# Gate buffers ordered by their whole size, the scratch of the weight sums in another place, and a floating place in PE's list for the spread maxima

## The chip, the cores and the metric

The kernel is one program on 1 core of one Trainium2 chip. The metric is the device time of one execution in microseconds (us); the time of a kernel is the median of its runs. PE is the matrix engine, DVE the vector engine, ACT the scalar engine, POOL the GpSimd engine and SP the engine that issues the DMAs. L1263 is line 1263 of the kernel before; where the changed kernel has other line numbers, the text still speaks of lines of the kernel before, unless it says otherwise.

## The reference

Three parts run one after the other in float32. The attention has 4 batches, 8 heads, 576 positions and 64 features a head; the two dense parts work on its 4 x 576 = 2304 tokens of 512 features.

```python
def _attn_ref(q, k, v, s):
    scores = scale * np.matmul(q, k.transpose(0, 1, 3, 2))
    cum = np.cumsum(np.maximum(s, 0.0), axis=-1)
    bias = -(cum[:, :, :, None] - cum[:, :, None, :])
    scores = np.where(causal, -1000000000.0, scores + np.minimum(bias, 0.0))
    attn = softmax(scores)
    return np.matmul(attn, v)

def _moe_ref(x, w_in, w_out):        # 512 -> 2048 -> 512
    h = x @ w_in
    g = h * np.cos(h)
    return g @ w_out

def _moe2_ref(x, w1, w2, w3, w_out): # 512 -> 768 -> 512
    h = np.maximum(np.maximum(x @ w1, x @ w2), x @ w3)
    return h @ w_out
```

## The kernel before

**How the order comes about.** The program adds operations to a list planner (`P.add`): each with an engine, a planned duration, a key, and the byte spans that it reads and writes. Overlapping spans become dependences. The planner then simulates the engines with these durations and puts, whenever an engine is free, the ready operation of the smallest key on its list. Each engine issues its list in that order and waits at the head of it, so a late operand holds up everything behind. `P.flex` adds an operation with several choices of engine; each choice carries a number of microseconds by which it counts as ready later than it is. The evacuations (L891) choose in this way between ACT (L893) and DVE (L895). Matmuls of PE that are given through `link` keep the order in which they were linked.

**Operands.** A float32 operand is scaled by a power of two and split into two float16 halves, high and low; a product is three matmuls (high x high, high x low, low x high). ACT writes the high half (L402 for gates, L501 for operands) and DVE the low half (L432, L504).

**The power of two (`power`, L475).** The largest magnitude of each of 128 partitions is reduced on DVE (L479), cut to its power (L482, L485) and put on a diagonal (L488, into one buffer `dip_b`); PE multiplies that by ones (L491), so that all partitions see all maxima, and DVE reduces the bank (L494) and inverts (L496). This chain is called a spread of the maxima here. It is used in attention, for the gates (`gate_scale`), for each token block (`x_operands`, L1113) and each half of the weights (`w_operands`, L1156).

**The stages.** Attention runs in 32 steps. Beside its last ones PE computes h = x w_in in blocks of 320 or 256 tokens (L922, the projection); L893 on ACT evacuates it into one of three buffers `hs_b`, and SP stores it to the DRAM tensor `h_dram` (L440).

The gate stage (L1224) follows. It runs over five slabs of tokens, slab 0 of 256 and slabs 1 to 4 of 512, and in each over 16 chunks of h, one of 128 of the 2048 features. A chunk is loaded from `h_dram` (into one of 5 buffers `hl_b`); ACT rounds h / 2 pi to an integer (L1244, 3 buffers `kq_b`), DVE takes the remainder (L1246, 5 buffers `gl_b`), ACT the sine (L1249), DVE multiplies by h (L1252); L402 and L432 make the halves (8 buffers `gh_b`); PE runs 12 matmuls into four banks that it keeps for the whole slab (L1263). At a slab's end the banks are evacuated to `x2_b` by L893 or L895.

In between stand pieces for the next stage. `w_value` loads a piece of the third layer's weights, from 64-bit words, and rebuilds the values on DVE (L449, L452, L455) in one of three buffers `val_b`, with a maximum (L1152). `w_operands` makes the sums of weight pieces (L1167) in a scratch `ws4_b` and their halves (L501, L504). `x_operands` takes the maxima of a token block (L1118), the differences (L1128, scratch `sum_b`) and the halves. In slab 2 `w_operands(0)` and `x_operands(0)` stand side by side.

The product stage computes x w1, x w2 and x w3 by a scheme of 7 products in place of 8, in 27 groups (weight half, token block, which w). A product is 6 matmuls of 384 columns (L1336); ACT keeps the first ones of a group (L1344), DVE adds the others to them (L1361). The second and third `w_operands` and the last `x_operands` stand inside it. The last product with the second w_out (L1300) ends the kernel.

**Memory.** `hl_b`, `kq_b`, `gl_b` and `gh_b` are cut out of memory in which attention kept probabilities and exponentials, in pieces of 2048 bytes; of slab 0 only the first 1024 bytes of each are in use. `val_b` and `ws4_b` lie over x operands and over the three store buffers `hs_b` of h: the third of `val_b` over the one whose store is the last, `ws4_b` over the other two. The lines that decide it:

```python
    sum_b = place(3 * 4 * TB).parts(3)
    val_b = [Buf(nc, tail0 + 4096 * m, 4096) for m in range(3)]
    ws4_b = Buf(nc, tail0 + 3 * 4096, 3072)
    ...
            hs_, ks_, ls_ = ([z.span(0, 4 * n)] for z in (hb, kb, lb))
```

Of the kernel before, what the change touches and what calls it, by code (L numbers as in the profile page):

```python
# [13 lines left out]
BF16 = mybir.dt.bfloat16  # L14
# [17 lines left out]
NC2 = DFF2 // 128  # L32
# [8 lines left out]
TB = 384  # L41
# [280 lines left out]
def attn_moe_kernel(ctx, tc, qT, kT, v, s, w_in, w_out, w1, w2, w3, wo2, out):  # L322
    nc = tc.nc
# [7 lines left out]
    P = Plan()  # L331
# [24 lines left out]
    wg_b = [alloc(32) for _ in range(NC1 // G)]  # L356
# [3 lines left out]
    tail0 = used[0]  # L360
    x_b = [alloc(NPAIR * 2 * RANGES[r][1] * 2).ring(NPAIR) for r in range(2)]
    hs_b = alloc(3 * 2560).ring(3)
    tail1 = used[0]
# [15 lines left out]
    warm_b = alloc(256)  # L379
    dip_b = alloc(256)  # L380
# [93 lines left out]

    def power(col, given, small, key, z, unit=2.0 ** -14):  # L475


        a, sp, o, os_ = small.ap(F32, 8), [small.span()], bank(z)[:, 0:128], [bspan(z)]
# [11 lines left out]
            op0=ALU.mult), reads=sp + [eye_b.span()], writes=[dip_b.span()])  # L490
        P.add("PE", 0.07, key, lambda: nc.tensor.matmul(  # L491
            o, warm_b.ap(BF16, 128), dip_b.ap(BF16, 128), start=True, stop=True),
            reads=[warm_b.span(), dip_b.span()], writes=os_)
# [94 lines left out]
    for h in range(2):  # L588
        z = tri[64 * h:128, S - 64:]
# [425 lines left out]
    for st in range(len(STEPS)):  # L1015
# [16 lines left out]
        if st in WI_AT:  # L1032
            i_ = WI_AT.index(st)
            for c in range(NC1 * i_ // len(WI_AT), NC1 * (i_ + 1) // len(WI_AT)):
# [4 lines left out]
                small = wg_b[c // G]  # L1039
# [30 lines left out]
    def place(size):  # L1070
        z = Buf(nc, low[0], size)
        low[0] += size
        assert low[0] <= low_end
        return z
# [3 lines left out]
    w0_b, xo_b, xo1_b = place(WB), place(XB), place(XB)  # L1078
    sum_b = place(3 * 4 * TB).parts(3)
    val_b = [Buf(nc, tail0 + 4096 * m, 4096) for m in range(3)]  # L1080
    ws4_b = Buf(nc, tail0 + 3 * 4096, 3072)
    assert 3 * 4096 + 3072 <= tail1 - tail0
    gates0 = rest_b[0].lo
# [29 lines left out]
    def x_operands(tp, key, z):  # L1113
# [3 lines left out]
        for i in range(4):  # L1117
# [3 lines left out]
                reads=[x2_b[tp].span(8 * TB * i, 8 * TB)], writes=[small.span()])  # L1121
        power(4, small, small, key, z, 2.0 ** -12)
        by, bsp = small.ap(F32, 8)[:, 7:8], [small.span()]
# [32 lines left out]
    def w_operands(fp, key, z):  # L1156


        small = mn_b[fp]
        power(6, wg_b[fp], small, key, z, 2.0 ** -12)  # L1160
        by, bsp = small.ap(F32, 8)[:, 7:8], [small.span()]
# [22 lines left out]
    def out_values(key):  # L1184

        top, small = am_b[0], am_b[1]
        for f in range(NC2):
# [10 lines left out]
                reads=[top.span(), mn_b[f // 2].span()], writes=[top.span()])  # L1198
        power(NC2, top, small, key, 7)

# [23 lines left out]
    for t in range(-(-NT // 512)):  # L1224
# [5 lines left out]
        for c in range(NC1):  # L1230
# [9 lines left out]
            gt, lr, gs_, gl_s = two(gb, n)  # L1240
            hs_, ks_, ls_ = ([z.span(0, 4 * n)] for z in (hb, kb, lb))
            load(ht, h_dram[:, c, col0:col0 + n], 512 * n, key - 3,
# [210 lines left out]
T0_BANKS = 1  # L1453
WO_FROM = 8
WO_KEY = 300
WM_KEY = 200
# [83 lines left out]
```

## Time and profile before

| | us |
|---|---|
| median of 3 runs (lowest, highest) | 845.21 (842.23, 846.32) |
| the profiled execution: time | 843.37 |
| its span from first to last instruction | 841.6 |
| PE busy | 798.6 (95%) |
| DVE busy | 691.0 (82%) |
| ACT busy | 542.8 (64%) |
| POOL busy | 51.1 (6%) |

The profiled execution's own time is 1.8 us over its span, and its mean granted clock was 0.984 of full speed. It is 1.84 us under the median of the runs.

Two views are used ahead of the result. A row of the instructions in order of time gives start, length, engine, line, operation, output<-input with their sizes, and how many instructions of the kind ran one behind the other; in brackets stand the idle time of the engine before the row and what ended it. SPq is SP issuing a DMA. A row's length reaches some 0.08 us into the next row's, since instructions are pipelined; from start to start is the step. A row of busy time by stretch gives the stretch, its length, the busy time (and the instructions) of PE, PE's weight loads, DVE, ACT and POOL, then the granted clock of PE, the share of time of the DMA engines and GB/s.

### The profile page before, as it was taken

To read this page: it belongs to the slowest core of one execution; us is meant where nothing else is said; L and a number is where in the kernel's file an instruction comes from. 1 tells how busy PE (TensorE), PEld (TensorE's weight loads), DVE (VectorE), ACT (ScalarE), POOL (GpSimd) and SP (SyncE) were. 2 spreads that over 40 slices of the span, in tenths; PEclk is the share of its full clock that TensorE was granted. 3 is DMA by queue.
4 is the path that set the end of the run, shared out by engine and by line. 5 is a ranking of instruction groups with operands and counts; after the bars stand their busy time and mean duration, and the time that the engine had idled before them with its cause. 6 is when DMAs were issued, how large, how long until landed. Compare 5 with 4: busy or idle time off the path is not lost.

```text
span 841.6 us, 16200 instructions
## 1 busy us (share of the span) xinstructions
PE 798.6 (95%) x5905; PEld 504.1 (60%) x5905; DVE 691.0 (82%) x1677; ACT 542.8 (64%) x1173; POOL 51.1 (6%) x80
## 2 busy tenths in 40 slices
PE   7988589999999999899997989999999999999998
PEld 4666466788778768778543434444566666555554
DVE  7999989987987898588999999999999999613120
ACT  2787778988888889458976789962562533322121
POOL 4511112001000100000000000000000000000000
PEclk9899989999999999999999899999999999999999
DMA  8689978999999999955453134403003120010112
GB/s 250 141 192 220 220 184 223 223 210 216 240 175 211 240 172 221 263 167 167 140 160 113 51 101 128 148 13 125 26 1 100 51 90 12 1 42 35 38 38 75
DMA packets 154571, 114.14 MB, mean 136 GB/s; under 512 B 109662, under 2 KB 132446, under 8 KB 154492
## 3 DMA queue, kind: packets, MB, share of 16 engines
q1 hardware_dynamic: 154492, 113.11, 53.6%
q8 instruction: 46, 0.75, 0.4%
q14 instruction: 33, 0.27, 0.1%
HBM read 63.13 MB, written 23.74 MB: 103 GB/s over the span
## 4 chain that ended last, share of the span: by engine, by line
PE 50%; DVE 32%; DMA 7%; ACT 5%; issue 3%; SPq 1%; POOL 1%; POOLq 0%; DVEq 0%; ACTq 0%
PE banks L1336 21%; PE banks L922 14%; PE banks L1300 8%; DVE p L432 8%; DVE p L1252 4%; DVE p L1246 4%; PE banks L708 3%; PE banks L774 3%; DVE p L721 3%; DVE p L504 2%; ACT p L402 2%; DMA p<-h_dram 2%; DVE p L452 2%; DVE p L455 1%; DMA p<-in_moe_w_out_dram 1%
## 5 line engine op out<-in xcount | busy, mean ns | idle before, releaser
L922 PE MATMUL banks<-p,p 128*128 128x256 f16 (+1 forms) x1536 | 204.6, 289 | 13.1 <-ACT p L893 5.1
L1263 PE MATMUL banks<-p,p 128*128 128x512 f16 (+1 forms) x960 | 189.9, 360 | 2.5 <-DVE p L432 1.4
L1336 PE MATMUL banks<-p,p 128*128 128x384 f16 x1134 | 185.6, 326 | 1.1 <-DVE p L485 1.1
L922 PEld LDWEIGHTS <-p 128*128 128x128 f16 x1536 | 146.0, 99 | 61.6 <-issue 14.9
L402 ACT ACTIVATE p<-p,p 128x512 f16<-128x512 f32 (+4 forms) x241 | 143.1, 625 | 48.1 <-DVE p L1252 16.6
L432 DVE SCALAR_TENSOR_TENSOR p<-p,p,p 128x512 f16<-128x512 f32 (+4 forms) x244 | 153.7, 656 | 11.1 <-ACT p L402 10.4
L1263 PEld LDWEIGHTS <-p 128*128 128x128 f16 x960 | 94.3, 98 | 103.1 <-issue 12.5
L1336 PEld LDWEIGHTS <-p 128*128 128x128 f16 x1134 | 110.8, 98 | 74.9 <-issue 1.3
L893 ACT ACTIVATE p<-banks,p 128x256 f32<-128x256 f32 (+2 forms) x166 | 84.8, 520 | 100.2 <-PE banks L1300 61.6
L727 ACT ACTIVATE p<-p,p 128x128 f32<-128x128 f32 (+4 forms) x144 | 82.9, 576 | 19.4 <-DVE p L721 17.7
L1344 ACT ACTIVATE p<-banks 128x384 f32<-128x384 f32 x90 | 43.9, 488 | 73.2 <-PE banks L1336 71.7
L721 DVE CUSTOM_DVE_ANT_0 p<-banks,p 128x128 f32<-128x128 f32 (+4 forms) x144 | 71.6, 512 | 2.2 <-POOL p L417 0.5
L1300 PE MATMUL banks<-p,p 128*128 128x512 f16 (+1 forms) x342 | 71.0, 368 | 0.0
L1361 DVE TENSOR_TENSOR p<-banks,p 128x384 f32<-128x384 f32 x81 | 44.0, 550 | 30.7 <-PE banks L1336 30.3
L501 ACT ACTIVATE p<-p,p 128x512 f16<-128x512 f32 (+2 forms) x73 | 54.1, 783 | 15.9 <-DVE p L1167 3.9
L504 DVE SCALAR_TENSOR_TENSOR p<-p,p,p 128x512 f16<-128x512 f32 (+2 forms) x73 | 59.0, 830 | 6.0 <-ACT p L501 6.0
L1300 PEld LDWEIGHTS <-p 128*128 128x128 f16 x342 | 33.5, 98 | 36.1
L1249 ACT ACTIVATE p<-p,p 128x512 f32<-128x512 f32 (+1 forms) x80 | 51.6, 669 | 5.3 <-DVE p L1246 5.2
L708 PE MATMUL banks<-r,r 64*128 64x256 f32 (+3 forms) x360 | 48.3, 345 | 2.6 <-DVE p L721 1.4
L1252 DVE TENSOR_TENSOR p<-p,p 128x512 f32<-128x512 f32 (+1 forms) x80 | 49.1, 632 | 0.6 <-ACT p L1249 0.6
L1246 DVE SCALAR_TENSOR_TENSOR p<-p,p 128x512 f32<-128x512 int32 (+1 forms) x80 | 48.8, 631 | 0.0
L1244 ACT ACTIVATE p<-p 128x512 int32<-128x512 f32 (+1 forms) x80 | 44.5, 575 | 2.7 <-DMA p<-h_dram 2.5
(100 smaller groups left out, 776.1 us busy)
## 6 DMA issues: line engine op xcount, KB each, us to landing
p<-h_dram SPq DMA_DIRECT2D x64, 256.0 KB
p<-in_moe_w_out_dram SPq DMA_DIRECT2D x22, 512.0 KB
h_dram<-p SPq DMA_DIRECT2D x32, 320.0 KB
p<-in_moe_w_dram SPq DMA_DIRECT2D x18, 512.0 KB
p<-in_moe_w_in_dram SPq DMA_DIRECT2D x16, 512.0 KB
h_dram<-p SPq DMA_DIRECT2D x32, 256.0 KB
p<-in_k_dram SPq DMA_DIRECT2D x16, 288.0 KB
out_dram<-p SPq DMA_DIRECT2D x17, 256.0 KB
```

Source lines behind the costliest of these rows:

```text
L402: "ACT": (slow(cols, 0.19 if par else 0.09), lambda: nc.scalar.activation(out=out, in_=src, func=AF.Copy, scale=by)),
L432: n = P.add("DVEP", dve1(cols) + 0.06, key, lambda: nc.vector.scalar_tensor_tensor(out=lo, in0=src, scalar=by, in1=hi, op0=ALU.mult, op1=A ...
L504: P.add("DVEP", dve1(cols) + 0.06, key, lambda: nc.vector.scalar_tensor_tensor(out=lo, in0=src_, scalar=by, in1=hr, op0=ALU.mult, op1=ALU. ...
L721: nc.vector.tensor_tensor_reduce(out=e, in0=sc, in1=km, op0=ALU.add, op1=ALU.min, scale=-0.125, scalar=3.0e38, accum_out=mn[:, j:j + 1]),
L727: "ACT", act(n, 0.28), tg, lambda j=j, e=e, mn=mn, sm=sm: nc.scalar.activation(out=e, in_=e, func=AF.Exp, scale=-1.0, bias=mn[:, j:j + 1], ...
L893: "ACT": (act(cols, 0.05 if by is None else 0.15), lambda: nc.scalar.activation(out=out, in_=src, func=AF.Copy, scale=1.0 if by is None el ...
L922: nc.tensor.matmul(hp, w[:, wp, ks], xx, start=(k == 0 and m == 0), stop=(k == KD - 1 and m == 2),)
L1246: P.add("DVEP", dve1(n), key, lambda kt=kt, ht=ht, lt=lt: nc.vector.scalar_tensor_tensor(out=lt, in0=kt, scalar=-TWO_PI, in1=ht, op0=ALU.m ...
L1252: P.add("DVEP", dve1(n), key, lambda ht=ht, lt=lt: nc.vector.tensor_tensor(out=lt, in0=lt, in1=ht, op=ALU.mult), reads=hs_ + ls_, writes=ls_)
L1263: nc.tensor.matmul(bank(base + d)[:, 0:n], w[:, wp, ds], xx, start=(c == 0 and z == 0), stop=(c == NC1 - 1 and z == 2))
L1300: nc.tensor.matmul(o, hv[hp], wv[:, wp, c0:c1], start=(f == 0 and m == 0), stop=(f == NC2 - 1 and m == 2))
L1336: nc.tensor.matmul(bank(z)[:, 0:TB], w_, x_, start=(opens and j == 0 and k == 0), stop=(j == 1 and k == 2), skip_group_check=True)
```

## The change

Three edits.

- In the gate stage the spans of the buffers of loaded h, of integers and of remainders (`hs_`, `ks_`, `ls_`) are the whole 2048 bytes in each slab, not the part that a chunk fills. Only slab 0 fills less than the whole. Its operations are ordered behind whatever attention kept in the second half of a buffer too.
- The scratch of the weight sums, `ws4_b`, is the first 3072 bytes of the scratch `sum_b` of the x operands, and no longer lies over `hs_b`.
- The matmul of a spread (L491) is added through `flex` with one engine and a margin: in the calls of `x_operands`, `w_operands` and `out_operands` the planner counts it as ready 2.0 us later than its operands are. The margin is 0 elsewhere. The instruction itself is the same.

The diff:

```diff
--- before.py
+++ after.py
@@ -472,7 +472,7 @@
         P.after(m, [rows_out, *after])
         return raw.ap(I64, cols).bitcast(I32).rearrange("p (n two) -> p n two", two=2)
 
-    def power(col, given, small, key, z, unit=2.0 ** -14):
+    def power(col, given, small, key, z, unit=2.0 ** -14, margin=0.0):
 
 
         a, sp, o, os_ = small.ap(F32, 8), [small.span()], bank(z)[:, 0:128], [bspan(z)]
@@ -488,8 +488,8 @@
         P.add("DVEP", dve2(128) + 0.06, key, lambda: nc.vector.tensor_scalar(
             out=dip_b.ap(BF16, 128), in0=eye_b.ap(F32, 128), scalar1=a[:, 5:6], scalar2=None,
             op0=ALU.mult), reads=sp + [eye_b.span()], writes=[dip_b.span()])
-        P.add("PE", 0.07, key, lambda: nc.tensor.matmul(
-            o, warm_b.ap(BF16, 128), dip_b.ap(BF16, 128), start=True, stop=True),
+        P.flex(key, [("PE", 0.07, lambda: nc.tensor.matmul(
+            o, warm_b.ap(BF16, 128), dip_b.ap(BF16, 128), start=True, stop=True), margin)],
             reads=[warm_b.span(), dip_b.span()], writes=os_)
         P.add("DVE", dve1(128), key, lambda: nc.vector.tensor_reduce(
             out=a[:, 6:7], in_=o, op=ALU.max, axis=AX.X), reads=sp + os_, writes=sp)
@@ -1076,10 +1076,10 @@
     WB = 7 * 256 * 4 * 3
     XB = 7 * 2 * TB * 4
     w0_b, xo_b, xo1_b = place(WB), place(XB), place(XB)
-    sum_b = place(3 * 4 * TB).parts(3)
+    sums = place(3 * 4 * TB)
+    sum_b, ws4_b = sums.parts(3), sums.part(0, 3072)
     val_b = [Buf(nc, tail0 + 4096 * m, 4096) for m in range(3)]
-    ws4_b = Buf(nc, tail0 + 3 * 4096, 3072)
-    assert 3 * 4096 + 3072 <= tail1 - tail0
+    assert 3 * 4096 <= tail1 - tail0
     gates0 = rest_b[0].lo
     xo2_b, w1_b = Buf(nc, gates0, XB), Buf(nc, gates0 + XB, WB)
     assert XB + WB <= 21 * 2048 <= const0 - e0
@@ -1119,7 +1119,7 @@
                 out=small.ap(F32, 8)[:, i:i + 1], in_=x2_b[tp].ap(F32, 2 * TB, 8 * TB * i), op=ALU.max,
                 axis=AX.X, apply_absolute_value=True),
                 reads=[x2_b[tp].span(8 * TB * i, 8 * TB)], writes=[small.span()])
-        power(4, small, small, key, z, 2.0 ** -12)
+        power(4, small, small, key, z, 2.0 ** -12, MARGIN)
         by, bsp = small.ap(F32, 8)[:, 7:8], [small.span()]
         for j in range(2):
             q = [x2_b[tp].part(16 * TB * j + 4 * TB * i, 4 * TB) for i in range(4)]
@@ -1157,7 +1157,7 @@
 
 
         small = mn_b[fp]
-        power(6, wg_b[fp], small, key, z, 2.0 ** -12)
+        power(6, wg_b[fp], small, key, z, 2.0 ** -12, MARGIN)
         by, bsp = small.ap(F32, 8)[:, 7:8], [small.span()]
         for m in range(3):
             v = [val_b[m].part(1024 * i, 1024) for i in range(4)]
@@ -1196,7 +1196,7 @@
             P.add("DVE", 0.07, key, lambda col=col, unit=unit: nc.vector.tensor_tensor(
                 out=col, in0=col, in1=unit, op=ALU.mult),
                 reads=[top.span(), mn_b[f // 2].span()], writes=[top.span()])
-        power(NC2, top, small, key, 7)
+        power(NC2, top, small, key, 7, margin=MARGIN)
 
     def out_operands(key):
 
@@ -1238,7 +1238,7 @@
             hb, kb, lb, gb = take("hl", hl_b), take("kq", kq_b), take("gl", gl_b), take("gh", gh_b)
             ht, kt, lt = hb.ap(F32, n), kb.ap(I32, n), lb.ap(F32, n)
             gt, lr, gs_, gl_s = two(gb, n)
-            hs_, ks_, ls_ = ([z.span(0, 4 * n)] for z in (hb, kb, lb))
+            hs_, ks_, ls_ = ([z.span()] for z in (hb, kb, lb))
             load(ht, h_dram[:, c, col0:col0 + n], 512 * n, key - 3,
                  reads=[dspan(u, c // 2) for u in sources], writes=hs_)
             P.add("ACT", act(n), key, lambda kt=kt, ht=ht: nc.scalar.activation(
@@ -1452,6 +1452,7 @@
 BES_BANK = 6
 T0_BANKS = 1
 WO_FROM = 8
+MARGIN = 2.0
 WO_KEY = 300
 WM_KEY = 200
 SC_KEY = 5.0
```

**Where instructions move.** On DVE, where slab 0's gates begin and the last stores of h are still under way. A name p_2048_226 is a buffer of 2048 bytes a partition; p_3072_253 is `ws4_b`, p_4096_247 to p_4096_249 are `val_b`, p_64_228 is the gates' scale. Before:

```order
L432 SCALAR_TENSOR_TENSOR p_2048_239<-p_2048_238,p_64_228,p_2048_239 128x256
L432 SCALAR_TENSOR_TENSOR p_2048_242<-p_2048_241,p_64_228,p_2048_242 128x256
L1246 SCALAR_TENSOR_TENSOR p_2048_231<-p_2048_225,p_2048_229 128x256
L1167 TENSOR_TENSOR p_3072_253<-p_4096_247 128x256
L1252 TENSOR_TENSOR p_2048_226<-p_2048_226,p_2048_224 128x256
L1246 SCALAR_TENSOR_TENSOR p_2048_235<-p_2048_230,p_2048_233 128x256
L1252 TENSOR_TENSOR p_2048_231<-p_2048_231,p_2048_229 128x256
```

and now:

```order
L432 SCALAR_TENSOR_TENSOR p_2048_227<-p_2048_238,p_64_228,p_2048_227 128x256
L1246 SCALAR_TENSOR_TENSOR p_2048_226<-p_2048_230,p_2048_224 128x256
L432 SCALAR_TENSOR_TENSOR p_2048_232<-p_2048_241,p_64_228,p_2048_232 128x256
L1246 SCALAR_TENSOR_TENSOR p_2048_231<-p_2048_234,p_2048_229 128x256
L1252 TENSOR_TENSOR p_2048_226<-p_2048_226,p_2048_224 128x256
L449 TENSOR_SCALAR p_4096_249<-p_4096_134 128x512
L1246 SCALAR_TENSOR_TENSOR p_2048_235<-p_2048_225,p_2048_233 128x256
L1252 TENSOR_TENSOR p_2048_231<-p_2048_231,p_2048_229 128x256
```

The first L1167 stood between the first remainders of slab 0; it now stands some 160 rows further down, in slab 2, and writes another buffer. L449, which writes the third of `val_b`, now stands between the remainders of slab 0.

On PE, in slab 2, the two L491 of `w_operands(0)` and `x_operands(0)` (difference from before to now, minus is before). A chunk is 24 rows here, a weight load and a matmul 12 times; p_2048_239, p_2048_242, p_2048_244 and p_2048_245 are buffers of `gh_b` with the gates of chunks 3, 4, 6 and 7 of the slab:

```order
 L1263 LDWEIGHTS p_2048_143
 L1263 MATMUL banks<-p_2048_239,p_2048_143 128x512
-L491 LDWEIGHTS p_256_68
-L491 MATMUL banks<-p_256_762,p_256_68 128x128
 L1263 LDWEIGHTS p_2048_146
 L1263 MATMUL banks<-p_2048_242,p_2048_146 128x512
```

and further on:

```order
 L1263 LDWEIGHTS p_2048_130
 L1263 MATMUL banks<-p_2048_244,p_2048_130 128x512
+L491 LDWEIGHTS p_256_68
+L491 MATMUL banks<-p_256_761,p_256_68 128x128
 L1263 LDWEIGHTS p_2048_131
 L1263 MATMUL banks<-p_2048_245,p_2048_131 128x512
```

The L491 between chunks 3 and 4 is gone from there. One between chunks 4 and 5 is in both lists; it was the second of the two and is now the first. The second now stands between chunks 6 and 7.

On DVE, in the same slab, from the low half (L432) of chunk 10 to that of chunk 11; the 8 gate buffers let DVE run that far ahead of PE. p_21504_250 and p_21504_252 are the finished operands of x and of the weights, p_32_95 and p_32_96 the columns of their spreads. Before, 12 of the 15 rows:

```order
L432 SCALAR_TENSOR_TENSOR p_2048_236<-p_2048_235,p_64_228,p_2048_236 128x512
L1246 SCALAR_TENSOR_TENSOR p_2048_238<-p_2048_230,p_2048_237 128x512
L504 SCALAR_TENSOR_TENSOR p_21504_252<-p_4096_247,p_32_95,p_21504_252 128x512 x2
L504 SCALAR_TENSOR_TENSOR p_21504_252<-p_3072_253,p_32_95,p_21504_252 128x768
L504 SCALAR_TENSOR_TENSOR p_21504_252<-p_4096_248,p_32_95,p_21504_252 128x512
L1167 TENSOR_TENSOR p_3072_253<-p_4096_248 128x256
L504 SCALAR_TENSOR_TENSOR p_21504_252<-p_4096_249,p_32_95,p_21504_252 128x512
L1167 TENSOR_TENSOR p_3072_253<-p_3072_253,p_4096_248 128x256
L1167 TENSOR_TENSOR p_4096_248<-p_4096_248 128x256
L1167 TENSOR_TENSOR p_3072_253<-p_4096_248,p_3072_253 128x256
L1252 TENSOR_TENSOR p_2048_238<-p_2048_238,p_2048_237 128x512
L1246 SCALAR_TENSOR_TENSOR p_2048_241<-p_2048_234,p_2048_240 128x512
```

and now, all six rows:

```order
L432 SCALAR_TENSOR_TENSOR p_2048_236<-p_2048_235,p_64_228,p_2048_236 128x512
L494 TENSOR_REDUCE p_32_96<-banks 128x1
L488 TENSOR_SCALAR p_256_761<-p_512_307,p_32_95 128x128
L496 RECIPROCAL p_32_96<-p_32_96 128x1
L1252 TENSOR_TENSOR p_2048_241<-p_2048_241,p_2048_240 128x512
L432 SCALAR_TENSOR_TENSOR p_2048_239<-p_2048_238,p_64_228,p_2048_239 128x512
```

The weight sums and halves that stood between the gates of chunks 10 and 11 stand further down now; in their place one spread ends (L494, L496) and the other begins (L488).

## Rows read from the trace of the kernel before

**Rows 1.** Busy time by stretch, the gate stage.
```profile
440.00:460.00 20.00, 16.90 (x79) 7.55 (x77) 20.00 (x36) 15.22 (x25) 0.00 (x0) 1.00 0.48 143
500.00:520.00 20.00, 20.00 (x94) 9.07 (x93) 19.39 (x32) 18.88 (x32) 0.00 (x0) 1.00 0.41 119
```

**Rows 2.** Instructions in order of time, PE alone, slabs 0 to 3.
```profile
383.98 72.92 PE L1263 MATMUL banks<-p,p 128*128 128x256 f16 x432
463.06 0.26 PE L491 MATMUL banks<-p,p 128*128 128x128 bf16 x1 [6.17 <-DVE p L488]
463.12 4.90 PE L1263 MATMUL banks<-p,p 128*128 128x512 f16 x12
...
491.80 8.36 PE L1263 MATMUL banks<-p,p 128*128 128x512 f16 x38 [0.68 <-DVE p L432]
```

**Rows 3.** Instructions in order of time, PE, then DVE, at the product stage's start.
```profile
582.48 8.94 PE L1336 MATMUL banks<-p,p 128*128 128x384 f16 x54
592.50 1.14 PE L1336 MATMUL banks<-p,p 128*128 128x384 f16 x6 [1.08 <-DVE p L485]
591.90 0.55 DVE L1361 TENSOR_TENSOR p<-banks,p 128x384 f32<-128x384 f32 x1
593.03 0.28 DVE L488 TENSOR_SCALAR p<-p,p 128x128 bf16<-128x128 f32 x1
```

**Rows 4.** PE after an earlier wait: order of time, then busy time by stretch.
```profile
356.86 2.07 PE L774 MATMUL banks<-p,p 128*64 128x256 f16 x54 [3.29 <-DMA p<-h_dram]
359.00:361.00 2.00, 2.00 (x8) 1.00 (x7) 1.52 (x4) 1.61 (x5) 0.00 (x0) 0.50 0.31 79
```

**Rows 5.** Instructions in order of time, all engines and SP's DMA issues, slab 0.
```profile
382.74 0.37 SPq L440 DMA_DIRECT2D h_dram<-p  x1
...
387.76 0.42 DVE L1167 TENSOR_TENSOR p<-p 128x256 f32<-128x256 f32 x1 [3.40 <-DMA h_dram<-p]
...
388.55 0.51 ACT L402 ACTIVATE p<-p,p 128x256 f16<-128x256 f32 x1 [3.22 <-DVE p L1252]
388.97 0.51 ACT L893 ACTIVATE p<-banks,p 128x320 f32<-128x320 f32 x1
...
389.59 0.42 SPq L440 DMA_DIRECT2D h_dram<-p  x1
...
399.06 0.42 DVE L449 TENSOR_SCALAR p<-p 128x512 int32<-128x512 int32 x1
```

**Rows 6.** Instructions in order of time, DVE: one of each kind.
```profile
454.72 0.74 DVE L895 TENSOR_SCALAR p<-banks,p 128x512 f32<-128x512 f32 x1
...
486.01 0.42 DVE L1167 TENSOR_TENSOR p<-p,p 128x256 f32<-128x256 f32 x1
...
487.01 0.74 DVE L504 SCALAR_TENSOR_TENSOR p<-p,p,p 128x512 f16<-128x512 f32 x1
487.67 0.69 DVE L1246 SCALAR_TENSOR_TENSOR p<-p,p 128x512 f32<-128x512 int32 x1
488.27 1.01 DVE L504 SCALAR_TENSOR_TENSOR p<-p,p,p 128x768 f16<-128x768 f32 x1
489.20 0.68 DVE L1252 TENSOR_TENSOR p<-p,p 128x512 f32<-128x512 f32 x1
```

**Rows 7.** Instructions in order of time, DVE: an L488, and L432 of five chunks.
```profile
463.87 0.28 DVE L488 TENSOR_SCALAR p<-p,p 128x128 bf16<-128x128 f32 x1
...
491.01 0.74 DVE L432 SCALAR_TENSOR_TENSOR p<-p,p,p 128x512 f16<-128x512 f32 x1
...
493.48 0.75 DVE L432 SCALAR_TENSOR_TENSOR p<-p,p,p 128x512 f16<-128x512 f32 x1
...
495.34 0.74 DVE L432 SCALAR_TENSOR_TENSOR p<-p,p,p 128x512 f16<-128x512 f32 x1
...
496.61 0.75 DVE L432 SCALAR_TENSOR_TENSOR p<-p,p,p 128x512 f16<-128x512 f32 x1
...
498.47 0.74 DVE L432 SCALAR_TENSOR_TENSOR p<-p,p,p 128x512 f16<-128x512 f32 x1
```

## The prediction

> **What bounds the kernel now.** I read the busy time by stretch first, to see which engine is full where, then PE and DVE in order of time, then the printed order. A slab is up to 512 tokens of the gate stage, a chunk one of its 16 groups of 12 matmuls; I write s2c13 for chunk 13 of slab 2. From 440 to 460 us DVE is busy all 20 us and PE is not; from 500 to 520 PE is full, with 94 matmuls in 20 us [rows 1], so a matmul takes 0.213 us and a chunk 2.56 us. PE runs without a hole from 383.98 to 456.9; it then waits 6.17 us for DVE's L488 at the head of its list, and its next 12 matmuls take 4.90 us, twice the usual [rows 2]. At 491.80 PE waits for the last time for a gate and then goes on: the 38 matmuls are the rest of s2c13, s2c14, s2c15 and three of s3c0. So s3c0 begins at 491.8 + 35 x 0.213 = 499.3 and s3c2 at 504.4. PE has no idle time from there to the last matmul but 1.08 us at 592.50 [rows 3]. The end is therefore set by when PE gets to s3c2, and by that one hole. How long PE stands at L488 matters only as far as gates are ready behind it.
>
> **The change part by part, on the profiled execution (843.37 us, 1.84 under the median of the runs).**
>
> *Whole-size gate buffers.* Only two buffers get new neighbours: s0c2's loaded h and its integer buffer now wait for the last probabilities. The load leaves with those of c3 and c4 instead of before them, and its L1246 moves some 17 places down DVE's list, to about 369 us. Its gate is needed by PE's third chunk, after 386. No instruction is added, one weight load passes the h load on SP's queue, POOL's list is the same: nothing, hidden under PE's projection of the last block, which ends at 383.98 [rows 2]. If that cover went, PE would wait for one h load at the head of the stage, as it did for 3.29 us in the projection before [rows 4].
>
> *Scratch of the weight sums.* L1167 stands early in DVE's list and waits 3.40 us for a store of h; ACT waits 3.22 us behind it [rows 5]. Both go. What is late next: DVE's L449 on the third value buffer, which lies over the buffer of the very last h store. L449 is at 399.06 now [rows 5]; in the new list 14 operations of 256 columns fewer stand ahead of it, at 0.34 each by L1167's step [rows 6], 4.8 us, and the 3.40 is gone, so DVE comes to it at 390.9. The last evacuation L893 starts at 388.97 now; without the 3.22, and with two ACT operations of 0.4 newly ahead, it starts at 386.55, and its store is issued 0.62 later, at 387.2. The store issued at 382.74 let L1167 start at 387.76 [rows 5]: 5.0 us. So this one releases L449 at 392.2, and DVE waits 1.3 us of the 3.40 again. I take 2.1 us gained on DVE; bounds 0 and 3.4.
> The Trainium skill (DMA: Bandwidth & Descriptors, "Anatomy of one DMA") fits a DMA on another issue path as about 2.0 us and bytes at 436 GB/s, an estimate of 2.8 us for this store of 328 KB, under which L449 would wait for nothing and the whole sum below would be 5.4 us; the same section warns that a write to HBM can be long in being confirmed. The row has 5.0, and I go by it.
>
> *DVE's order in slab 2.* A row overlaps the next by 0.08, so the steps are 0.33 for L1167, 0.66 for L895, L432 and the 512-column L504, 0.93 for the 768-column one, 0.60 for L1246 and L1252 [rows 6]. Ahead of s2c13's L432 the new list has four L1167, two L1246, one L895, two wide and two narrow L504 fewer: 1.3 + 1.2 + 0.7 + 1.9 + 1.3 = 6.4 us. For s2c14 it is 3.45, for s2c15 2.46. Ahead of s3c0's it has one L895 fewer, but two L1246 and one L1252 more: 1.14 us later; for s3c1 1.27 later. With the 2.1 from above, and the ends of these L432 now (start of each plus 0.66, [rows 7]): s2c13 483.2, s2c14 488.6, s2c15 491.4, s3c0 496.3, s3c1 498.3.
>
> *PE's list.* The first L491 of slab 2 stands one chunk later, the second two more chunks. PE reaches them at 459.5 and 464.8. DVE's L488 for them: the first ends at 463.0 now, has 1.3 us less ahead, and gains 2.1: 459.6. The second starts at 463.87 [rows 7], ends 0.2 later, has 2.3 more ahead: 464.3. So neither wait is worth speaking of: the 6.17 us go, and the slow 12 matmuls with them. PE then finishes s2c12 at 480.3 and is at DVE's gates: it waits 2.9 us for s2c13, 2.8 for s2c14, 0.2, and 2.3 for s3c0, which begins at 496.3 (now 499.3). s3c1 follows at 498.9, s3c2 at 501.4 against 504.4: **3.0 us gained**, half of the 6.17; the rest comes back as waits for gates.
>
> *Start of the product stage.* PE's 1.08 is put down to L485, which begins as the evacuation L1361 of 591.90 to 592.45 ends; the matmul opens the bank that L1361 reads. Ahead of that L1361 the new list has four L1167 and two L895 fewer and one L452 (0.6) more: 2.1 us, and 2.1 from above: it ends at 588.3. PE is ready for that matmul at 591.42 now (592.50 less 1.08), and 3.0 earlier at 588.4. **1.1 us gained**, bounds 0 and 1.1. The L491 behind it moves from 60 to 78 matmuls into the stage, to 592.3 (18 matmuls and the six of the row, at 8.94 / 54 = 0.166); its L488 (593.03, [rows 3], 1.5 less ahead) is done at 589.7. The next L491 now stands 24 matmuls further, 4.0 us, instead of 120; DVE does seven wide L504 after it instead of before, so it should be in time; were it not, up to 1 us. Evacuations moved from DVE to ACT (two L895) lie on an ACT that is idle there.
>
> Sum: 3.0 + 1.1 = 4.1 us; 843.37 becomes 839.3, and from the median of the runs, 845.21, **841.1 us**.
>
> **The rivals.** 0.5% is 4.2 us here, about what a measurement of this kernel tells from no change.
> *A, the store's wait does not come back.* If L449 finds its buffer free, s3c0 starts at 495.0 and s3c2 at 500.1: 4.3 + 1.1 = 5.4, 839.8 us. For it: the last evacuation may come sooner than I have it; against: 5.0 us for a store [rows 5].
> *B, the whole 3.40 comes back there or elsewhere on DVE.* s3c0 at 498.4, s3c2 at 503.5: 0.9 + 1.1 = 2.0, 843.2 us. For it: DVE is full, and what it gains early it can lose to ACT; against: no other store is outstanding.
> *C, PE's clock falls in the new gaps and stays down.* After the 6.17 us wait [rows 2] and after one of 3.29 [rows 4] PE worked at 1.2 GHz (granted 0.50); now gaps of 2.9 and 2.8 stand a chunk apart. At that level a chunk takes twice 2.56, 5.12 us (the row has 4.90). One or two chunks cost nothing, since the gates are late anyway; three put s3c0 at 498.8, total 1.6. From the fourth on it loses: with s2c13 to s3c2 all at half, six chunks, s3c3 begins at 514.2 instead of 507.0, 7.2 lost less 1.1, and the kernel takes 851.3 us. Against it: the fall behind the longest wait lasted 12 matmuls, and the 38 behind the last wait of 0.68 ran at full rate, 0.22 each [rows 2].
> That gaps between groups of matmuls can make the clock go up and down through a whole stretch is in the Trainium skill (TensorE: Matmul & The Clock Gate, "A second HAM failure mode: psum-queue depth-cycling"). No stretch of this trace shows it; by that rule C is the outcome.
> *D, it does nothing:* the gates of s3c0 stay where they were and the 1.08 comes back at the moved L491: 845.2 us.
>
> **How the numbers follow.** Forecast 0.38 (with the ends of its bounds), A 0.22, B 0.14, C 0.13, D 0.13. My forecast lies on the edge of 0.5%, so that about half of it, 0.19, joins A's 0.22 on the faster side: 0.41. Slower by over 0.5% is C, 0.13. The rest, 0.46, is within: the other half of the forecast, B and D. Range 838.0 (A with 1.8 us of scatter, less than the 3.0 between the lowest run and the median) to 846.5 (D with 1.3, a little over the 1.1 between the median and the highest run): it leaves out C and the far end of A.
>
> **What would show it.** Right: no L1167 waiting for a store near 387; L449 waiting 1 to 2 us near 391; PE without a wait at L491 in 455 to 466, but short waits for L432 between 480 and 497; s3c2 near 501.5; no hole in PE from there on. Wrong: a granted clock of 0.50 past 497 (C); PE already waiting before 480, which would say that DVE's list runs later than counted; or a new wait of PE on DVE or ACT after 580.

## The result and the profile after

The changed kernel takes 836.12 us (median of 6 runs, 835.00 to 838.69), the kernel before 844.38 in the same comparison (6 runs, 842.23 to 846.33). The ratio is 0.9907, with a 95% interval of 0.9882 to 0.9931: some 8 us faster, twice the forecast 4.1, and 1.9 us under the low end of the forecast's range. The forecast counted from 845.21, the median of the three runs known then; that accounts for 0.8 us of the 5.0 between 841.1 and 836.12. The profiled execution:

```profile
PE 794.9 (95%) x5905; PEld 503.0 (60%) x5905; DVE 689.1 (83%) x1675; ACT 543.2 (65%) x1175; POOL 50.8 (6%) x80
```

PE is busy for 3.7 us less than before, and DVE for 1.9 us less; the counts of PE's instructions are the same. PE in order of time (columns as in [rows 2]), from the row behind the last but one L774 group of attention to the product stage:

```profile
343.57 8.51 PE L922 MATMUL banks<-p,p 128*128 128x256 f16 x72
352.02 1.81 PE L774 MATMUL banks<-p,p 128*64 128x256 f16 x54
...
355.13 0.30 PE L922 MATMUL banks<-p,p 128*128 128x320 f16 x1 [0.79 <-ACT p L787]
356.00 13.47 PE L922 MATMUL banks<-p,p 128*128 128x320 f16 x98 [0.57 <-DVE p L792]
370.60 0.22 PE L491 MATMUL banks<-p,p 128*128 128x128 bf16 x1 [1.14 <-DVE p L488]
...
380.61 75.51 PE L1263 MATMUL banks<-p,p 128*128 128x256 f16 x444
455.96 0.22 PE L491 MATMUL banks<-p,p 128*128 128x128 bf16 x1
...
461.19 0.22 PE L491 MATMUL banks<-p,p 128*128 128x128 bf16 x1
...
478.38 0.38 PE L1263 MATMUL banks<-p,p 128*128 128x512 f16 x1 [1.42 <-ACT p L402]
479.23 2.53 PE L1263 MATMUL banks<-p,p 128*128 128x512 f16 x11 [0.48 <-DVE p L432]
482.84 0.38 PE L1263 MATMUL banks<-p,p 128*128 128x512 f16 x1 [1.08 <-ACT p L402]
484.63 5.39 PE L1263 MATMUL banks<-p,p 128*128 128x512 f16 x23 [1.41 <-DVE p L432]
491.20 0.38 PE L1263 MATMUL banks<-p,p 128*128 128x512 f16 x1 [1.18 <-ACT p L402]
492.37 56.02 PE L1263 MATMUL banks<-p,p 128*128 128x512 f16 x251 [0.79 <-DVE p L432]
...
576.77 12.84 PE L1336 MATMUL banks<-p,p 128*128 128x384 f16 x78
```

Four things differ from before.

First, the last 54 matmuls of L774 start at 352.02 with no wait ahead of them, where PE stood 3.29 us in the kernel before [rows 4]. Second, the gate stage therefore begins earlier, at 380.61 against 383.98 [rows 2]. Counted from the L774 group before (343.57 here; 345.06 before, the row behind that group in both), that is 37.04 instead of 38.92: 1.88 us. The other 1.49 are there before anything of the change has run: the profiled execution was ahead by that much already. Of the 3.29, smaller waits behind it take 2.50 back (0.79, 0.57, 1.14), and the projection no longer runs its first part at the lower clock level [rows 4].

Third, both L491 of slab 2 pass without a wait (455.96, 461.19; before 6.17, [rows 2]), and PE waits for gates instead: 1.90 us for s2c13, 2.49 for s2c14, 1.97 for s3c0. After the last of these it works for a while at the lower level. Busy time by stretch (columns as in [rows 1]):

```profile
490.00:494.00 4.00, 2.03 (x7) 0.77 (x6) 4.00 (x8) 4.00 (x8) 0.00 (x0) 0.83 0.63 186
494.00:498.00 4.00, 4.00 (x16) 1.58 (x14) 4.00 (x8) 4.00 (x8) 0.00 (x0) 0.75 0.27 78
```

The granted clock is 0.83 and 0.75 between 490 and 498, and 1.00 in the 4 us before and behind. The 251 matmuls from 492.37 take 56.02 us, 0.2232 each, where the 275 in the same place before took 59.51, 0.2164 each: the difference is 1.7 us. Fourth, the hole of 1.08 us at the start of the product stage [rows 3] is gone: 78 matmuls run through from 576.77 to the L491, which does not wait either.

DVE in the same execution:

```profile
387.97 0.43 DVE L449 TENSOR_SCALAR p<-p 128x512 int32<-128x512 int32 x1
...
478.43 0.75 DVE L432 SCALAR_TENSOR_TENSOR p<-p,p,p 128x512 f16<-128x512 f32 x1
...
483.83 0.74 DVE L432 SCALAR_TENSOR_TENSOR p<-p,p,p 128x512 f16<-128x512 f32 x1
...
486.69 0.75 DVE L432 SCALAR_TENSOR_TENSOR p<-p,p,p 128x512 f16<-128x512 f32 x1
...
491.57 0.75 DVE L432 SCALAR_TENSOR_TENSOR p<-p,p,p 128x512 f16<-128x512 f32 x1
```

L449 on the third value buffer (387.97) starts without a wait. The four L432 behind it are those of s2c13, s2c14, s2c15 and s3c0.

### The profile page after: what moved, and what is told of

It is laid out like the page before. It is cut to its first block, busy times and chain, and to the rows that moved or that the text cites. A ratio compares the mean times of both kernels' runs of the same rounds, so it can differ in the third digit from the quotient of the medians.

```text
span 834.7 us, 16175 instructions
## 1 busy us (share of the span) xinstructions
PE 794.9 (95%) x5905; PEld 503.0 (60%) x5905; DVE 689.1 (83%) x1675; ACT 543.2 (65%) x1175; POOL 50.8 (6%) x80
## 4 chain that ended last, share of the span: by engine, by line
PE 56%; DVE 28%; DMA 8%; ACT 4%; issue 3%; POOL 1%; SPq 0%; DVEq 0%; ACTq 0%; POOLq 0%
PE banks L1336 22%; PE banks L1263 10%; PE banks L922 9%; PE banks L1300 8%; DVE p L432 7%; PE banks L708 3%; DVE p L1246 3%; DMA p<-in_moe_w_out_dram 3%; DVE p L1252 3%; DVE p L721 2%; PE banks L774 2%; DVE p L504 2%; DMA p<-in_v_dram 2%; ACT p L402 1%; DVE p L452 1%
## 5 line engine op out<-in xcount | busy, mean ns | idle before, releaser
L1263 PE MATMUL banks<-p,p 128*128 128x512 f16 (+1 forms) x960 | 189.9, 360 | 6.5 <-ACT p L402 3.7
L432 DVE SCALAR_TENSOR_TENSOR p<-p,p,p 128x512 f16<-128x512 f32 (+4 forms) x244 | 153.9, 655 | 11.4 <-ACT p L402 10.7
L1263 PEld LDWEIGHTS <-p 128*128 128x128 f16 x960 | 94.2, 98 | 101.1 <-issue 10.6
```

Source lines behind the costliest of these rows:

```text
L432: n = P.add("DVEP", dve1(cols) + 0.06, key, lambda: nc.vector.scalar_tensor_tensor(out=lo, in0=src, scalar=by, in1=hi, op0=ALU.mult, op1=A ...
L1263: nc.tensor.matmul(bank(base + d)[:, 0:n], w[:, wp, ds], xx, start=(c == 0 and z == 0), stop=(c == NC1 - 1 and z == 2))
```

## What the wait at L774 was

In the kernel before, the chain of work that ended last (start, length, what) runs through that wait:

```profile
353.13 0.02 SPq L440
...
353.19 3.62 DMA p<-h_dram
...
356.86 2.07 PE banks L774 x54
```

SP issues a load of h at 353.1 and PE starts L774 when it has landed. The built program says why. The third buffer of loaded h lies at bytes 169856 to 171904 of a partition, as the program counts them; the transposed last probabilities begin at 171136, in the same buffer's last 768 bytes. The load of s0c2 fills only 169856 to 170880, and the planner, which was told only of these 1024 bytes, put it ahead of the last L774. But the waits in the program are made by named buffers, and L774, which comes later in the list and reads an overlapping buffer, was made to wait for the load: its first weight load waits for a DMA counter to reach 560, the count that this load brings. In the changed kernel the planner knows of the whole 2048 bytes, the load stands behind the last L774 and waits for it, and the same weight load waits for 528, the transposition that it needs.

## The experiments

The theories, as the expectations name them: P and T, that the spans free PE from a wait for a load of h at the last L774, and that the rest follows from it; Q and Q2, that this wait or the earlier start is nothing of the change; R, S and U, that the scratch gives nothing, the margin gives all, or the edits add; V and W, on what is left in slab 2.

s3c0 below is the start of slab 3's first matmul on PE, less the start of the last but one L774 group (343.31 before). That takes out most of what differs between executions before the change acts. It is read from the trace, as the start of the first of the 192 matmuls (L1263) of that slab: 499.35 - 343.31 = 156.0 before.

| kernel | edits | median us | ratio, 95% interval | wait at last L774 | at L1167 | first L491 of slab 2 | s3c0 |
|---|---|---|---|---|---|---|---|
| before | none | 844.38 | 1 | 3.29 | 3.40 | 6.17 | 156.0 |
| changed | all three | 836.12 | 0.9907 (0.9882 to 0.9931) | 0 | none there | 0 | 149.4 |
| e1_spans | spans | 835.51 | 0.9908 (0.9880 to 0.9936) | 0 | 0.61 | 1.71 | 148.4 |
| e2_scratch | scratch | 838.72 | 0.9949 (0.9927 to 0.9970) | 3.06 | none there | 1.12 | 151.5 |
| e3_margin | margin | 843.95 | 1.0005 (0.9980 to 1.0030) | 3.03 | 3.86 | 4.69 | 160.8 |
| e4_no_spans | scratch, margin | 839.50 | 0.9955 (0.9932 to 0.9978) | 3.34 | none there | 0 | 152.5 |
| e5_no_scratch | spans, margin | 834.67 | 0.9905 (0.9876 to 0.9935) | 0 | 0.59 | 0 | 146.8 |
| e6_no_margin | spans, scratch | 834.86 | 0.9896 (0.9864 to 0.9927) | 0 | none there | 2.00 | 149.1 |
| e8_swap | another piece | 836.55 | 0.9925 (0.9896 to 0.9954) | 0 | 0.60 | 1.58 | 149.7 |
| c1_x_later | all, x later | 831.16 | 0.9856 (0.9828 to 0.9884) | 0 | 0 | 0 | 141.3 |
| c2_x_later_m0 | c1, margin 0 | 832.44 | 0.9873 (0.9844 to 0.9902) | 0 | 0 | 0 | 142.2 |

"None there" says that no L1167 stands in slab 0. Each ratio is against the kernel before on the same chip; its median there was 844.38 for the changed kernel, 843.67 for e1 to e4, 843.08 for e5 to c2 and 843.53 for e8.

**The spans alone (e1_spans).**

```diff
-            hs_, ks_, ls_ = ([z.span(0, 4 * n)] for z in (hb, kb, lb))
+            hs_, ks_, ls_ = ([z.span()] for z in (hb, kb, lb))
```

> Only the whole-size spans of the gate buffers, on the kernel before. Theory P (the last probabilities' product waited for a load of h): in the kernel before, the last 54 matmuls of L774 wait 3.29 us for a load of h; here they do not. Counted from the L774 group ahead of it (345.06 minus 1.75 before), the first gate matmul comes 38.9 us behind the end of that group before, and here 36 to 37.5. The loss of 6.17 us at L488 in slab 2 stays between 5 and 7, since DVE is earlier by the same amount, and the kernel is 1.5 to 3.3 us faster, 841 to 843 against 844.4. Rival Q (the earlier start of the gate stage in the profile of the changed kernel is scatter between executions): the wait or one as long stays, 38.9 us stay within 0.5, and the time is the same within 1 us.

The wait for the load is gone, and the first gate matmul comes 36.8 us behind the start of the L774 group before (379.75 - 342.92), where before has 40.7 (383.98 - 343.31). Counted as in the expectation, from the row behind that group, it is 35.1 against 38.9, earlier than the 36 to 37.5 expected. Rival Q falls. But the gain is 8 us and not 1.5 to 3.3, and the wait at L488 did not stay. PE, then SP and DVE, with the store out of a buffer under the scratch:

```profile
353.11 1.81 PE L774 MATMUL banks<-p,p 128*64 128x256 f16 x54
...
379.75 72.92 PE L1263 MATMUL banks<-p,p 128*128 128x256 f16 x432
454.38 0.23 PE L491 MATMUL banks<-p,p 128*128 128x128 bf16 x1 [1.71 <-DVE p L488]
...
474.86 5.12 PE L1263 MATMUL banks<-p,p 128*128 128x512 f16 x23 [1.85 <-DVE p L432]
482.17 0.38 PE L1263 MATMUL banks<-p,p 128*128 128x512 f16 x1 [2.19 <-ACT p L402]
483.72 59.51 PE L1263 MATMUL banks<-p,p 128*128 128x512 f16 x275 [1.17 <-DVE p L432]
```

```profile
379.27 0.37 SPq L440 DMA_DIRECT2D h_dram<-p  x1
...
381.96 0.42 DVE L1167 TENSOR_TENSOR p<-p 128x256 f32<-128x256 f32 x1 [0.61 <-DMA h_dram<-p]
```

The gain is larger than PE's wait because that wait also held up DVE, the engine that is full behind it. Busy time by stretch (columns as in [rows 1]), from the start of the last but one L774 group to DVE's first L488 of slab 2, in the kernel before, in e1 and, for the next experiment, in e2:

```profile
343.31:462.74 119.43, 110.30 (x789) 70.49 (x789) 103.31 (x220) 85.33 (x168) 0.00 (x0) 0.98 0.54 165
342.92:454.04 111.12, 109.21 (x789) 69.69 (x788) 101.50 (x218) 86.26 (x169) 0.00 (x0) 1.00 0.59 177
343.23:457.49 114.26, 110.41 (x789) 70.65 (x788) 101.18 (x214) 86.14 (x169) 0.00 (x0) 0.99 0.59 172
```

In e1 DVE reaches L488 8.31 us sooner. It is busy for 1.81 us less (one L895 of 0.74 fewer stands there; the rest is not separated) and idle for 9.62 us instead of 16.12. These 6.50 us lie almost wholly in two places. The first is L792, which waits for ACT's L787, which waits for L774. Before, then e1:

```profile
359.44 0.49 DVE L792 SCALAR_TENSOR_TENSOR p<-banks,p 128x320 f16<-128x320 f32 x1 [3.84 <-ACT p L787]
355.44 0.49 DVE L792 SCALAR_TENSOR_TENSOR p<-banks,p 128x320 f16<-128x320 f32 x1 [0.23 <-ACT p L787]
```

That is 3.61 us. The second is L1167, which waits 0.61 us for a store instead of 3.40 [rows 5], 2.79 us. Both DVE and the store are some 3 us earlier in e1; what shrinks is the time from the store's issue to L1167, 2.7 us here (381.96 - 379.27) and 5.0 before. A load of 512 KB of weights is issued 1.2 us ahead of this store before, and 0.7 us behind it in e1. Before, then e1:

```profile
381.58 0.33 SPq L440 DMA_DIRECT2D p<-in_moe_w_dram  x1
379.98 0.33 SPq L440 DMA_DIRECT2D p<-in_moe_w_dram  x1
```

e3 has the order of before and 5.5 us, e5 and e8 have the order of e1 and 2.7; no run changes this order alone. L491 of slab 2 is passed at 454.38 where it was 463.06.

**The scratch alone (e2_scratch).**

```diff
-    sum_b = place(3 * 4 * TB).parts(3)
+    sums = place(3 * 4 * TB)
+    sum_b, ws4_b = sums.parts(3), sums.part(0, 3072)
-    ws4_b = Buf(nc, tail0 + 3 * 4096, 3072)
```

> Only the move of the scratch of the weight sums, on the kernel before. Theory P: DVE's 3.40 us at L1167 go, no other wait for a store takes their place (L449 found its buffer free in the changed kernel), PE's wait at L488 in slab 2 falls from 6.17 to about 2.8 to 4, the gates behind come 2 to 3.4 us earlier, and the kernel is 2 to 3.4 us faster, 841 to 842.4. PE's wait for a load of h ahead of the last L774 stays at about 3.3. Rival R (what DVE gains there it loses to ACT or to L449 within slab 0): L488 is reached as late as before within 1 us, and the time is the same within 1 us.

```profile
457.82 0.23 PE L491 MATMUL banks<-p,p 128*128 128x128 bf16 x1 [1.12 <-DVE p L488]
```

The wait for the load stays (3.06), the one at L1167 is gone, and PE's wait at L488 falls to 1.12, further than expected. The gain is 4.3 us (0.51%, interval 0.30 to 0.73%), where 2 to 3.4 were expected. No wait for a store took L1167's place, so rival R falls. L488 itself came 5.25 us earlier (457.49 against 462.74), 1.85 more than the 3.40. The third stretch above tells why: on the way there DVE is idle for 3.0 us less than before (13.08 against 16.12), and busy for 2.1 us less, since four L1167 and one L895 fewer stand ahead of L488.

**The margin alone (e3_margin).** The change without its first two edits.

```diff
-        P.add("PE", 0.07, key, lambda: nc.tensor.matmul(
-            o, warm_b.ap(BF16, 128), dip_b.ap(BF16, 128), start=True, stop=True),
+        P.flex(key, [("PE", 0.07, lambda: nc.tensor.matmul(
+            o, warm_b.ap(BF16, 128), dip_b.ap(BF16, 128), start=True, stop=True), margin)],
```

> Only the margin of the spreads, on the kernel before. Theory P: PE's 6.17 us at L488 go, but DVE is as late as before, so they come back as waits for L402 and L432 of s2c13 to s3c0, 9 us or more in sum, with the clock at its lower level for a while; s3c0 starts within 1.5 us of the 499.3 of before. The hole of 1.08 us at the start of the product stage goes. The kernel is the same within 2 us. Rival S (the margin is what made the kernel faster): 5 us or more faster, 839.5 or less.

```profile
465.91 0.27 PE L491 MATMUL banks<-p,p 128*128 128x128 bf16 x1 [4.69 <-DVE p L488]
```

The time is the same, as theory P said, and rival S falls. The way there is another than expected: the L491 one chunk further down still waits 4.69 us for L488, because DVE is that late. By the table s3c0 comes 4.7 us later than before, where within 1.5 was expected; the profiled execution took 846.04 us, 2.1 over the median of its kernel. The hole at the product stage's start is gone here as forecast.

**The change without the spans (e4_no_spans).**

```diff
-            hs_, ks_, ls_ = ([z.span()] for z in (hb, kb, lb))
+            hs_, ks_, ls_ = ([z.span(0, 4 * n)] for z in (hb, kb, lb))
```

> The changed kernel with the spans of the gate buffers as they were before. Theory P: PE waits 3 to 3.6 us for a load of h ahead of the last L774, the gate stage starts 1.5 to 3 us later, and the kernel takes 837.6 to 839.5 us, against 836.1 for the whole change. Rival Q (the earlier start was scatter): 836 within 1 us.

```profile
359.11 3.25 PE L774 MATMUL banks<-p,p 128*64 128x256 f16 x54 [3.34 <-DMA p<-h_dram]
...
591.69 4.06 PE L1336 MATMUL banks<-p,p 128*128 128x384 f16 x24 [0.81 <-DVE p L482]
```

839.50 us, and the wait for the load is back at 3.34: theory P. These are the two edits on which the forecast rested its 4.1 us; together they give 3.8 (interval 1.9 to 5.7). A wait of 0.81 us is left at the product stage's start.

**The change without the scratch, and without the margin (e5_no_scratch, e6_no_margin).**

```diff
-    sums = place(3 * 4 * TB)
-    sum_b, ws4_b = sums.parts(3), sums.part(0, 3072)
+    sum_b = place(3 * 4 * TB).parts(3)
...
+    ws4_b = Buf(nc, tail0 + 3 * 4096, 3072)
```

```diff
-MARGIN = 2.0
+MARGIN = 0.0
```

> The changed kernel with the scratch of the weight sums where it was (spans and margin only). Theory T (the spans alone free PE at the last L774, and by the earlier stores of h also most of DVE's wait at L1167: 0.61 us were left of 3.40 with the spans alone): L1167 waits 0.3 to 1 us, and the kernel takes 835 to 838 us, as the spans alone do. Rival U (the three edits add): without the scratch's 0.5% it takes 840 or more.

> The changed kernel with a margin of 0 (spans and scratch only). Theory T: the spans have taken the scratch's gain already, so it takes 834 to 836.5 us, like the spans alone (835.5) and the whole change (836.1); PE waits 1 to 2 us at L488 and has 4 to 6 us of waits for gates in s2c7 to s3c0. Rival U (the gains of the single edits add): 844.4 x 0.9908 x 0.9949 = 832.4, at most 833.4.

DVE of the first, PE of the second:

```profile
381.65 0.43 DVE L1167 TENSOR_TENSOR p<-p 128x256 f32<-128x256 f32 x1 [0.59 <-DMA h_dram<-p]
```

```profile
455.05 0.23 PE L491 MATMUL banks<-p,p 128*128 128x128 bf16 x1 [2.00 <-DVE p L488]
...
477.85 0.38 PE L1263 MATMUL banks<-p,p 128*128 128x512 f16 x1 [1.79 <-ACT p L402]
478.99 5.14 PE L1263 MATMUL banks<-p,p 128*128 128x512 f16 x23 [0.76 <-DVE p L432]
485.21 0.38 PE L1263 MATMUL banks<-p,p 128*128 128x512 f16 x1 [1.08 <-ACT p L402]
486.26 56.92 PE L1263 MATMUL banks<-p,p 128*128 128x512 f16 x263 [0.68 <-DVE p L432]
```

Both take what the spans alone take; e5 lies 0.3 us under its range. Rival U's 840 is far above e5. For e6 the times alone do not decide: the sum of the single edits, 0.9857, lies just below its interval (0.9864 to 0.9927), but has an interval of its own, of some 0.0035 to either side by those of e1 and e2. The waits tell more. With the spans in, the scratch has 0.6 us of wait left to remove, and the margin turns the wait at L488 into longer waits for gates: without it PE waits 2.00 + 4.31 = 6.31 us in this stretch, with it 6.36 (the rows of the changed kernel), and s3c0 is at 149.1 and 149.4.

**The same wait taken away in another manner (e8_swap).** No span is changed; the piece of memory that lies half under the last probabilities becomes the last gate buffer.

```diff
-    hl_b, kq_b, gl_b, gh_b = (rest_b[a:b] for a, b in ((0, 5), (5, 8), (8, 13), (13, 21)))
+    free_b = rest_b[:2] + rest_b[3:] + rest_b[2:3]
+    hl_b, kq_b, gl_b, gh_b = (free_b[a:b] for a, b in ((0, 5), (5, 8), (8, 13), (13, 21)))
```

> The kernel before with its spans, scratch and spreads as they were; only one piece of 2048 bytes changes its role: the piece whose last 768 bytes lie under the last probabilities is the last gate buffer instead of the third buffer of loaded h, so that the load of s0c2 goes to a piece that lies under them as a whole. Theory T (that load, put ahead of the last L774, is what PE waited for): no wait for a load of h at the last L774, L1167 waits under 1 us, and the kernel takes 834.5 to 837.5 us like the spans alone (835.5). Rival Q2 (the wait at L774 is only what the profile names, and the spans worked through DVE's and ACT's order): the kernel stays above 840.

PE, then DVE (this kernel's lines are one further down from there on, so L1168 is L1167 of the others):

```profile
353.84 1.81 PE L774 MATMUL banks<-p,p 128*64 128x256 f16 x54
```

```profile
382.73 0.43 DVE L1168 TENSOR_TENSOR p<-p 128x256 f32<-128x256 f32 x1 [0.60 <-DMA h_dram<-p]
```

The last L774 does not wait, the store's wait is 0.60, and the time is that of e1 within the intervals. So what the spans do, they do by the place of that one load. The lists of SP and of every engine are the same as in e1, operation by operation, and differ from those of before from this place on, DVE's and ACT's too. e8 therefore does not tell the lost wait from the new order, which is a part of rival Q2. DVE's waits in e1 do so in part: 3.61 of the 6.50 us follow from L774's wait itself, and the 2.79 at L1167 go with the new order of SP.

**What is left in the gate stage (c1_x_later, c2_x_later_m0).** The operands of x move from slab 2 to slab 3, away from those of the weights.

```diff
-            if t in (2, 4) and c == 2:
-                x_operands(t // 2 - 1, key + 0.5, 4 * ((t + 1) % 2) + 3)
+            if t in (3, 4) and c == 2:
+                x_operands(t - 3, key + 0.5, 4 * ((t + 1) % 2) + 3)
```

> The changed kernel with x_operands(0) in slab 3 instead of slab 2. Theory V (what is left in the gate stage is DVE having the operands of weights and of x at once in slab 2: 6.4 us of PE waits for gates between 478 and 493 and 2.4 us at the lower clock behind them): the waits go down to 2 us or less, the product stage starts 5 to 8 us earlier than 576.8, and the kernel takes 828 to 832 us. Rival W (DVE has no slack in slab 3 either, 97% busy there): the waits come back in slab 3, and the time is 835 to 838.

> The same with a margin of 0. Theory V: like the one with the margin within 1.5 us, since the spread's place decides nothing where DVE is on time; a wait of PE at L488 of up to 2 us may stand in slab 2 or 3. Rival W: 835 to 838.

PE of c1:

```profile
448.39 41.60 PE L1263 MATMUL banks<-p,p 128*128 128x512 f16 x192
490.63 0.22 PE L491 MATMUL banks<-p,p 128*128 128x128 bf16 x1 [0.64 <-DVE p L895]
...
559.42 0.38 PE L1263 MATMUL banks<-p,p 128*128 128x512 f16 x1 [1.01 <-ACT p L402]
560.58 10.30 PE L1263 MATMUL banks<-p,p 128*128 128x512 f16 x47 [0.79 <-DVE p L432]
570.72 9.91 PE L1336 MATMUL banks<-p,p 128*128 128x384 f16 x60
```

Theory V holds. From 448 to 559 PE loses 0.64 us, where the changed kernel loses 6.36 and then 1.7 to the clock; what is left is 1.80 in slab 4. The product stage begins at 570.72 instead of 576.77. c1 takes 831.16 us; by the ratios that is 0.51%, 4.3 us, less than the whole change takes, and the two intervals meet at their ends (0.9884 and 0.9882). The planner's list differs in other places too: L1167 stands in slab 0 again, without a wait, so c1 is not a test of DVE's load alone. The margin again makes no difference that these runs tell.

## Why the prediction was wrong

**The step that failed** is the one on the whole-size gate buffers: "nothing, hidden under PE's projection of the last block". Alone it gives the whole gain. I followed the moved load down SP's queue and its remainder down DVE's list, and asked whether its gate would be late. I did not ask who waits for the load at the place that it leaves. The answer stood in my own rows: the 3.29 us of [rows 4] have a load of h as releaser, ahead of an L774 that reads none of h. I took that row as a measure for what a lost cover might cost, while it was the wait that the edit removes. What the runs showed in place of the zero: alone the edit is worth 8 us (0.9908), since the wait at L774 also held DVE for 3.61 us at L792, and L1167's wait falls from 3.40 to 0.61 with the new order of SP. The direction, faster, was right by luck: the scratch and the margin, on which the forecast rested it, give 3.8 us without the spans, but beside them nothing that these runs tell (0.9908 for the spans, 0.9907 for all three).

**The scratch.** L1167's wait went, as forecast. That L449 would wait 1.3 us of it again was wrong: in no run did L449 wait for a store. That is rival A's mechanism. Alone this edit gave 4.3 us, where A had 4.3 for the gate stage. The forecast took 5.0 us for a store from the one row of [rows 5]. That store is issued behind a load of 512 KB. In e1 a store of the same size, issued ahead of that load at 379.27, lets L1167 start at 381.96, 2.7 us later; and in the changed kernel the last store is issued at 383.65 and L449 runs at 387.97 without a wait, so this one took no more than 4.3. The estimate of 2.8 from the Trainium skill (DMA: Bandwidth & Descriptors, "Anatomy of one DMA"), whose fit is for another issue path, is near the row of e1. One row was too little to go by.

**DVE's order in slab 2** was right in its differences. The forecast ends of the L432 were 483.2, 488.6, 491.4 and 496.3; the rows give 479.1, 484.5, 487.3 and 492.2 (start plus 0.66). Each is 4.1 early. Of this, 1.49 is the lead that the profiled execution had before the change acts. The other 2.6 is for the most part DVE's idle time: from the last but one L774 group to the first L488 of slab 2 it is idle for 11.62 us here (113.45 less 101.83 busy) and for 16.12 before, 4.5 less, where the forecast had taken 2.1 less.

**PE's list.** No wait at L491, short waits for gates in its place: right, in kind and place. They sum to 6.36 us where 8.2 were forecast.

**The clock (rival C).** The mechanism is there, in small: behind the gaps of s2c14 and s3c0 the clock fell once, for a part of the 8 us from 490 to 498, and cost 1.7 us. By the rule of the Trainium skill (TensorE: Matmul & The Clock Gate, "A second HAM failure mode: psum-queue depth-cycling") it could go up and down through a whole stretch; this trace shows one fall. In e1, with waits of 1.85 us for s2c11 and 2.19 and 1.17 for s2c13, there is none; in e8, with the same list and the same waits within 0.01 us, there is one. e1, then e8:

```profile
482.00:486.00 4.00, 2.66 (x12) 1.17 (x12) 4.00 (x7) 2.84 (x6) 0.00 (x0) 1.00 0.30 94
482.00:486.00 4.00, 2.01 (x5) 0.64 (x5) 4.00 (x7) 2.85 (x6) 0.00 (x0) 0.73 0.36 123
```

So the length of these waits alone does not tell whether the clock falls.

**The product stage.** The hole of 1.08 went, as forecast, and the L491 moved to 78 did not wait. It hangs on the rest, though: e5 has 1.55 there and e6 1.18.

**The sum.** Without its wrong zero, the sum came near: e4, the change without the spans, gained 3.8 where the forecast for the same two edits was 4.1. In part that is luck, since two misses cancel: s3c0 came 3.5 us earlier (156.0 to 152.5) where 3.0 was forecast, and of the 1.08 at the product stage's start 0.81 was left. And the worth of the spans can't be added to that. The runs with the spans, whatever else they have (but for c1 and c2), and e8, reach s3c0 between 146.8 and 149.7; DVE is full up to there (20.00 of 20 us before, [rows 1], and 4.00 of 4 in the two stretches of the changed kernel), and a wait taken off PE comes back as one for gates. c1, which takes work from DVE in that slab, is the one that goes below.

## What to carry to other kernels

A load or a store that an edit moves has two sides: who needs its data later, and who waits for it where it stands now; a row whose releaser has nothing to do with what the waiting instruction reads is a dependence by place in memory, and worth a look at the addresses. A planner that counts bytes and a program that waits by named buffers disagree exactly where a buffer is used in part, and then an operation put early by the planner becomes a wait for those behind it. Where several edits feed one full engine, their single gains don't add; run each alone and each left out, and look for what that engine does in the stretch where it is full.

## What was not expected of the hardware

PE's first 18 matmuls took 5.83 us in the profiled execution before and 4.78 in the one after, though the lists of PE are the same there, and at 343 us 1.5 us of difference stood. A difference of 1 or 2 us between two profiles' absolute times is therefore no evidence by itself; the distance from a common row is.
